# First block of a two-stage expert kernel in whole float32 products, halves of its weights made one block later

## The chip, the cores and the metric

The kernel runs on one NeuronCore of one Trainium2 chip. Its engines are TensorE (PE, matrix products into PSUM; PEld is its weight load), VectorE (DVE), ScalarE (ACT), GpSimd (POOL) and SyncE (SP), which issues all DMAs here. The metric is the device time of one execution in microseconds.

## The reference

Inputs are `x` (8 batches, 8 heads, 512 rows, 64 wide) and `state` (8, 8, 32, 64) in float32, and five weight matrices that arrive as float64. Three stages follow one another:

```python
scores = scale * x @ state^T;  a  = softmax(scores);   xread = a @ state      # per batch and head
scores2 = scale * state @ x^T; a2 = softmax(scores2);  sread = a2 @ x
x = concat([xread, sread]) regrouped to rows of 512     # 8 batches of 512 rows, 8 x 32 rows of state
x = (silu(x @ w_gate) * (x @ w_val)) @ w_out            # 512 -> 1536 -> 512
out = gelu_like(x @ w2_in) @ w2_out                     # 512 -> 2048 -> 512
```

The output is 4352 rows of 512 in float32.

## The kernel before

**Halves.** A float32 number is held as two tiles of TensorE's reduced type fp32r: the high half (a rounding copy by ACT) and the rest (a subtract by DVE or POOL). A product of two such pairs is three matmuls: high by high, low by high, high by low (`mm_rows`, L252 to L257; `mm_in`; `out1`, L699 to L701).

**Blocks.** The first layer runs over nine blocks: batches 0 to 6, then the 256 rows of the state ("tail"), then batch 7. A block has 12 steps `f`. A step makes one gate product (`gv`), SiLU on ACT, one value product, their product on DVE (`sg`), cuts that into halves `h`, and adds the step before it to four output accumulators (`out1`, 12 matmuls). For a batch, the softmax weights `a` are not first multiplied with the state: `state_weights` multiplies the state with a unit of the gate and value weights (tile `wu`, four units k = 0 to 3 for each pair of steps u), in two groups g of four heads, and its result (`xh`, `xl`) is what the step's products use. In words: unit, state weights, products. `coming` places the state weights of the next pair of steps.

**Weights.** `stream` lists all weight units in the order in which they are needed: 24 gate/value units and 12 output units ("o") in block 0, and the 12 output units again in every later block. A unit of float64 is loaded as raw words by SP (512 KB), turned to float32 by two ACT instructions (`w_begin`, L193 and L194), two on DVE and one add on POOL (`w_join`, L206 to L210), and cut into halves by an ACT copy and a POOL subtract (`w_end`, L221 and L222). The float32 form of the output units is stored to DRAM (`w1o`) and only cut again in later blocks. The second layer's 32 units are turned in the same way in blocks 1 to 6, one at every odd step ("turn"), and stored for later. Four raw buffers hold what is under way. `need(key)` runs the stream up to a key, in program order.

**Order.** Each engine runs its instructions in the order in which the program is written. `START` lists the work ahead of the first step (attention of batch 0 in groups A0 and A1, and the first four units); `BLOCK0` puts batch 1's attention (G0, G1) and batch 0's state read into block 0 at (step, place); `GROUP` does the same for later blocks. In block 0 `w_beside` places beginnings ("B") and ends ("E") of units between the parts of a step.

Of the kernel before, what the change touches and what calls it, by code (L numbers as in the profile page):

```python
# [20 lines left out]
A0.load0 state0 A0.load1 weights1 A0.turn0 A1.load0 attn_state A0.turn_h0 A1.load1 weights2 A0.turn1  # L21
A0.turn_l0:v A0.turn_h1 A0.turn_l1:v A0.scores_apart0 A0.scores_apart1 begin A1.turn0 A0.max_n
A1.turn_h0 weights3 A0.less_max:p A1.turn1 A1.turn_h1 A1.turn_l0:v end A0.exp_n A1.turn_l1:v
A0.sum_n begin weights4 A0.over_sum:v A0.back end A0.a_h:a A0.a_l:v A1.scores_apart0 begin
A1.scores_apart1 A1.max_n sw0 A1.less_max:v end A1.exp_n begin A1.sum_n weights4 A1.over_sum:v A1.back
A0.max_s A1.a_h:a A1.a_l:v A1.max_s end sw1 G0.load A1.exp_s A0.exp_s state1
# [6 lines left out]
    (0, 2): "A1.turn_e A0.cut_x:v",  # L33
    (1, 0): "G0.turn0 G0.turn_h0 G0.turn_l0:v",
    (1, 1): "A1.cut_x:v",
    (1, 2): "A0.state_read",
    (2, 0): "A0.state_sum",
    (2, 1): "attn_state",
    (2, 2): "A1.state_read A1.state_sum",
# [3 lines left out]
    (4, 2): "G0.max_s G0.cut_x:v G0.less_max:v",  # L43
    (5, 0): "G0.exp_n",
    (5, 1): "G0.exp_s G0.sum_n",
    (5, 2): "G0.over_sum:v G1.load G0.back G0.turn_e",
    (6, 1): "G0.a_h:a G0.a_l:v",
    (6, 2): "G0.state_read",
    (7, 1): "G1.turn0 G1.turn_h0 G1.turn_l0:v",
    (7, 2): "G0.state_sum",  # L50
    (8, 0): "G1.scores0 G0.state_store",
    (8, 1): "G1.turn1 G1.turn_h1 G1.turn_l1:v",
    (8, 2): "G1.scores1",
    (9, 0): "G1.cut_x:v",
    (9, 2): "G1.max_s G1.max_n G1.less_max:v",
    (10, 0): "G1.exp_n next",
# [23 lines left out]
def kernel(  # L80
# [74 lines left out]
    held = set()  # L155
    joins = []
    units = {}
    pos = {"dma": 0, "begun": 0, "done": 0, "ahead": 4, "apart": False}
    RAWS = 4

# [4 lines left out]
    def w_dma(ahead=None):  # L165
        ahead = ahead or pos["ahead"]
        while pos["dma"] < pos.get("limit", len(stream)) and len(raws) + len(held) < ahead:
            key, src, _, _ = stream[pos["dma"]]
            if isinstance(src, tuple):
# [12 lines left out]
    def w_begin():  # L182
# [4 lines left out]
        t = raw = raws.pop(key)  # L187
        if isinstance(src, tuple) or src.dtype != F32:
            r = raw.bitcast(U32).rearrange("p (c t) -> p c t", t=2)
            hi, lo = r[:, :, 1], r[:, :, 0]  # L190
            t = work.tile([P, DM], F32, name="wt", tag="wt", bufs=3)
            tu = t.bitcast(U32)
            a.activation(t, hi.bitcast(F32), ACTF.Copy, scale=2.0**-112)  # L193
            a.activation(lo, lo, ACTF.Copy, scale=2.0**-29)  # L194
            joins.append((tu, hi, lo))
            if not pos["apart"]:
                w_join()
        else:
            held.add(key)
        temps[key] = t  # L200
        pos["begun"] += 1

    def w_join():
        while joins:
            tu, hi, lo = joins.pop()
            v.tensor_scalar(out=tu, in0=tu, scalar1=3, scalar2=None, op0=ALU.logical_shift_left)  # L206
            v.scalar_tensor_tensor(  # L207
                out=tu, in0=hi, scalar=0x80000000, in1=tu, op0=ALU.bitwise_and, op1=ALU.bitwise_or
            )
            pool_e.tensor_tensor(tu, tu, lo, op=ALU.add)  # L210

    def w_end():
        key, src, loc, keep = stream[pos["done"]]
        t = temps.pop(key)
        if loc is None:
            sy.dma_start(keep, t)
            pos["done"] += 1
# [10 lines left out]

    def w_step(lead=2):
# [4 lines left out]
        while pos["begun"] < min(pos["done"] + lead, len(stream)):  # L234
# [55 lines left out]

    def load_state(b):
# [9 lines left out]
    def attn_state(b):  # L301
# [4 lines left out]
        t = stz[b % 2]  # L306
        a.copy(t[:, :, HIGHS], pv[:, :, :, 0])
# [5 lines left out]
    class Group:  # L313


        def __init__(self, b, g, slots=None):
            self.b, self.g, self.slots = b, g, slots or {}

# [16 lines left out]
        def turn(self, q):  # L335
# [6 lines left out]
            self.xt[q] = ps, self.tile(f"xth{q}", [P, S], F32R), self.tile(f"xtl{q}", [P, S], F32R)  # L342

        def turn_h(self, q):
            a.copy(self.xt[q][1], self.xt[q][0])

        def turn_l(self, q, eng):
            ps, xh, xl = self.xt[q]
# [12 lines left out]
        def scores_apart(self, q):  # L361

            ST, st, xh, xl = self.for_scores(q)
            ps = at()[0:64]
            hi, lo = st[:, (1 - q) * 64 : (2 - q) * 64], st[:, q * 64 : q * 64 + 64]
            pe.matmul(ps, hi, xh, start=True, stop=False)
            pe.matmul(ps, lo, xh, start=False, stop=False)
            pe.matmul(ps, hi, xl, start=False, stop=True)
            a.copy(ST, ps)
# [54 lines left out]

        def a_h(self, eng):
            self.a = (ae, ao)[self.b % 2].tile([P, 2, S], F32R, name="a", tag=f"a{self.g}")
# [5 lines left out]
        def turn_e(self):  # L432
            self.ec = self.tile("ec", [P, J, 4, 64], F32R)
            ps = at()
            for j in range(J):
                pe.transpose(ps[:, j * P : (j + 1) * P], self.e2[:, j * P : (j + 1) * P], ident)
            cut(self.ec[:, :, 0:4:3], self.ec[:, :, 1:3], ps.rearrange("p (j q m) -> p j q m", j=J, q=2))

        def state_read(self):


            ps = at()
            for q in range(2):
# [10 lines left out]
        def state_sum(self):  # L454
            sm, ps = self.sm, self.sr
            low = ap.tile([P, P], F32, name="low", tag="low")
            self.srd = srd = ap.tile([P, D], F32, name="srd", tag="srd", bufs=2)
# [26 lines left out]
    def state_weights(b, u, g):  # L484
# [3 lines left out]
        pairs = []  # L488
        for q in range(2):
            sh, sl = (stz[b % 2][:, g, i + q : i + q + 2].rearrange("p c m -> p (c m)") for i in (1, 5))  # L490
# [6 lines left out]
    def mm_state(ps, b, f, t):  # L497

        c = slice(t * 2 * P + f % 2 * P, t * 2 * P + f % 2 * P + P)
        pairs = []  # L500
        for g in range(2):
# [12 lines left out]
    def plan_batch(plan, b):  # L514
# [11 lines left out]
        more = {"attn_state": lambda: attn_state(b), "next": load_next}  # L526
        if b == 1:
# [16 lines left out]
    def add_gv(u, k):  # L544
        r, c = slice(k * P, (k + 1) * P), slice(u * 2 * P, (u + 1) * 2 * P)
        add(("gv", u, k), (w_gate[r, c], w_val[r, c]), (wp, f"w{u * KD + k}", 1))
# [29 lines left out]
    for f in range(F1):  # L576
        add(("o", NB1 - 1, f), w1o[f], (wp, "o", 2))
        add(*next(rest), (wp, f"w{2 * f}", 1))
        add(*next(rest), (wp, f"w{2 * f + 1}", 1))
# [25 lines left out]
    def h_tile(n):  # L605
# [5 lines left out]
    names = ["xn", "xc0", "xc1", "xth0", "xtl0", "xth1", "xtl1", "ST", "sp", "aT", "e2", "ec"]  # L611
    far = {n: f"w{2 * F1 - 1 - i}" for i, n in enumerate(names)}
    A0 = Group(0, 0, {n: f"w{2 * F1 - 1 - len(names) - i}" for i, n in enumerate(["xn", "aT", "xth1", "xtl1"])})
    A1 = Group(0, 1, far)
    xop = {}
    groups[0, 0], groups[0, 1] = A0, A1
    groups[1, 0] = Group(1, 0)
# [3 lines left out]
        "begin": w_begin,  # L621
        "end": w_end,
# [41 lines left out]
    for i, blk in enumerate(order1):  # L664
# [5 lines left out]
        pos["apart"] = i > 0  # L670
# [19 lines left out]
        def out1(f, between=None, k0=0):  # L690
            if not acc:
                acc.extend(accs())
            need(("o", i, f))
            h = hs.pop(f)
            w = units.pop(("o", i, f))
            for e in range(KD):
                c = slice(e * P, (e + 1) * P)
                ps = acc[e][:, :N]
# [166 lines left out]
```

## Time and profile before

| | |
|---|---|
| three runs | 1671.36, 1671.38, 1673.2 us, median 1671.38 |
| profiled execution | 1668.41 us, span of the core 1666.6 us |
| PE busy | 1569.8 us of the span |
| mean granted clock of TensorE | 0.974 |

A span is the time from the first to the last instruction. The clock is given as a share of full speed (2.4 GHz). A matmul's row shows its latency; since matmuls follow one another in a pipeline, the price of one in a run of them is the distance from start to start.

### The profile page before, as it was taken

What the parts mean: (1) busy time and instruction counts of PE and PEld (TensorE: products, weight loads), DVE (VectorE), ACT (ScalarE), POOL (GpSimd) and SP (SyncE); (2) the same over time, 40 slices, a digit from 0 to 9 for tenths busy, and PEclk for the clock granted to TensorE, in tenths of its full rate; (3) what the DMA queues carried; (4) which work ended last, traced back from release to release, by engine and by line L of the source; (5) the groups of instructions that cost most, each with busy time, mean ns of one, the idle gap of its engine ahead of it and who ended that gap; (6) DMA issues with size and microseconds to landing.
All of it is one profiled execution on the core that took longest, in us unless ns stands there. A gap on an engine that the chain in (4) does not pass through costs nothing.

```text
span 1666.6 us, 18801 instructions
## 1 busy us (share of the span) xinstructions
PE 1569.8 (94%) x7100; PEld 1275.7 (77%) x7100; DVE 751.5 (45%) x1253; ACT 683.8 (41%) x1218; POOL 355.8 (21%) x263
## 2 busy tenths in 40 slices
PE   5677899999989999999999999999999999999997
PEld 3456677787777778779988888888888888888886
DVE  5787666564656666463233223222222222322222
ACT  5575555554545555454355222222222222222222
POOL 3565333233323323223354010000000000000000
PEclk7787899999999999999999999999999999999999
DMA  5345333423333343323243001010101010000000
GB/s 145 127 138 149 105 104 98 125 82 122 103 111 109 89 124 100 101 64 98 81 142 124 32 1 51 1 45 7 45 7 39 13 38 13 32 20 29 10 26 13
DMA packets 94963, 119.18 MB, mean 72 GB/s; under 512 B 45209, under 2 KB 54425, under 8 KB 94873
## 3 DMA queue, kind: packets, MB, share of 16 engines
q1 hardware_dynamic: 94872, 117.99, 23.4%
q8 instruction: 55, 0.90, 0.2%
q14 instruction: 36, 0.29, 0.1%
HBM read 88.08 MB, written 29.88 MB: 71 GB/s over the span
## 4 chain that ended last, share of the span: by engine, by line
PE 50%; DVE 0%; issue 0%
PE gv L250 8%; PE gv L249 8%; PE gv L248 8%; PE acc L261 7%; PE acc L260 7%; PE acc L262 7%; PE acc L701 1%; PE acc L700 1%; PE acc L699 1%; PE gv L256 1%; PE gv L255 1%; PE gv L257 1%; PE at L255 0%; PE at L256 0%; PE at L257 0%; DVE ev L602 0%
## 5 line engine op out<-in xcount | busy, mean ns | idle before, releaser
L826 DVE TENSOR_TENSOR sg<-gv,sg 128x512 f32<-128x512 f32 (+1 forms) x144 | 95.3, 662 | 433.3 <-ACT sg L825 433.3
L825 ACT ACTIVATE sg<-gv 128x512 f32<-128x512 f32 (+1 forms) x144 | 82.6, 573 | 447.3 <-PE gv L250 447.3
L222 POOL TENSOR_TENSOR wu<-raw,wu 128x512 fp32r<-128x512 f32 x128 | 178.8, 1402 | 278.5 <-ACT wu L221 203.0
L250 PE MATMUL gv<-xl,wu 128*128 128x512 f32 (+1 forms) x576 | 219.6, 381 | 0.0
L249 PE MATMUL gv<-xh,wu 128*128 128x512 f32 (+1 forms) x576 | 219.2, 381 | 0.0
L248 PE MATMUL gv<-xh,wu 128*128 128x512 f32 (+1 forms) x576 | 218.9, 380 | 0.0
L261 PE MATMUL acc<-wu,h 128*128 128x512 f32 x544 | 213.2, 392 | 0.0
L260 PE MATMUL acc<-wu,h 128*128 128x512 f32 x544 | 212.9, 391 | 0.0
L262 PE MATMUL acc<-wu,h 128*128 128x512 f32 x544 | 212.1, 390 | 0.0
L256 PE MATMUL gv<-a,xl 128*128 128x512 f32 x384 | 158.7, 413 | 15.7 <-DVE xl L590 12.4
L700 PE MATMUL acc<-h,wu 128*128 128x512 f32 (+1 forms) x432 | 166.1, 384 | 6.3 <-POOL wu L222 6.3
L699 PE MATMUL acc<-h,wu 128*128 128x512 f32 (+1 forms) x432 | 166.9, 386 | 0.0
L701 PE MATMUL acc<-h,wu 128*128 128x512 f32 (+1 forms) x432 | 165.1, 382 | 1.0 <-DVE h L757 0.9
L255 PE MATMUL gv<-a,xh 128*128 128x512 f32 x384 | 159.6, 416 | 0.5 <-ACT xh L589 0.5
L210 POOL TENSOR_TENSOR wt<-wt,raw 128x512 uint32<-128x512 uint32 x68 | 92.0, 1352 | 313.4 <-DVE wt L207 183.8
L257 PE MATMUL gv<-a,xh 128*128 128x512 f32 x384 | 157.3, 410 | 0.0
L590 DVE TENSOR_TENSOR h<-sg,h 128x512 fp32r<-128x512 f32 (+1 forms) x144 | 95.4, 663 | 95.4 <-ACT h L589 90.8
L589 ACT CAST h<-sg 128x512 fp32r<-128x512 f32 (+1 forms) x144 | 86.0, 597 | 104.9 <-DVE sg L826 104.9
L738 ACT ACTIVATE sg<-gv 128x512 f32<-128x512 f32 (+1 forms) x108 | 62.1, 575 | 159.7 <-PE gv L257 159.5
L248 PEld LDWEIGHTS gv<-xh,wu 128*128 128x128 f32 x576 | 108.3, 188 | 22.3
L249 PEld LDWEIGHTS gv<-xh,wu 128*128 128x128 f32 x576 | 108.1, 188 | 22.3
L250 PEld LDWEIGHTS gv<-xl,wu 128*128 128x128 f32 x576 | 108.3, 188 | 21.8
(105 smaller groups left out, 2590.7 us busy)
## 6 DMA issues: line engine op xcount, KB each, us to landing
raw<-w1o SPq DMA_DIRECT2D x96, 256.0 KB
raw<-in_moe_w_out_dram SPq DMA_DIRECT2D x28, 512.0 KB
raw<-in_moe_w_in_dram SPq DMA_DIRECT2D x16, 512.0 KB
y<-ev SPq DMA_DIRECT2D x16, 512.0 KB
xr<-y SPq DMA_DIRECT2D x32, 256.0 KB
out_dram<-ev SPq DMA_DIRECT2D x16, 512.0 KB
xn<-in_x_dram SPq DMA_DIRECT2D x14, 512.0 KB
raw<-in_moe_w_gate_dram SPq DMA_DIRECT2D x24, 256.0 KB
```

What stands on the lines that cost most here:

```text
L222: pool_e.tensor_tensor(u[:, 1, :], t, f32(u[:, 0, :]), op=ALU.subtract)
L248: pe.matmul(ps[:, :N], wh, xh, start=k == 0, stop=False)
L249: pe.matmul(ps[:, :N], wl, xh, start=False, stop=False)
L250: pe.matmul(ps[:, :N], wh, xl, start=False, stop=k == KD - 1)
L255: pe.matmul(ps, wh, xh, start=k == 0, stop=False)
L256: pe.matmul(ps, wl, xh, start=False, stop=False)
L260: pe.matmul(ps, lh, rh, start=first, stop=False)
L261: pe.matmul(ps, lh, rl, start=False, stop=False)
L262: pe.matmul(ps, ll, rh, start=False, stop=last)
L699: pe.matmul(ps, w[:, 0, c], h[:, 0, :N], start=f == 0, stop=False)
L700: pe.matmul(ps, w[:, 1, c], h[:, 0, :N], start=False, stop=False)
L701: pe.matmul(ps, w[:, 0, c], h[:, 1, :N], start=False, stop=f == F1 - 1)
```

## The change

In block 0 the products take float32 tiles as they are (`mm_whole`): one matmul instruction where there were three, and no halves are made of the units, of the state weights, of `a` or of `h`. That holds for the scores and the state read of batch 0 too (and for the state read of batch 1's first group). Units are begun and merged by `whole_slot`, three times a step; two gate/value units share one old slot of the halves. The halves of these 24 units are made later by `cut_unit` (one ACT copy, one POOL subtract): the first four in steps 8 to 10 of block 0, the other 20 in block 1, called from `coming` by `need(("cut", ...))`. State weights of the next pair are made ahead of the value product at odd steps and after it at even ones, as in later blocks. The second layer's units are turned at steps 3 to 9 of blocks 2 to 6, seven a block, and not at odd steps from block 1 on. `START` issues the loads of two weight units ahead of `x`.

```diff
 START = """
-A0.load0 state0 A0.load1 weights1 A0.turn0 A1.load0 attn_state A0.turn_h0 A1.load1 weights2 A0.turn1
-A0.turn_l0:v A0.turn_h1 A0.turn_l1:v A0.scores_apart0 A0.scores_apart1 begin A1.turn0 A0.max_n
...
+weights2 A0.load0 state0 A0.load1 A1.load0 A1.load1 weights4 A0.turn0 attn_state A0.turn_h0 A0.turn1
+A0.turn_h1 A0.scores_full slot A1.turn0 A1.turn_h0 A1.turn1 A1.turn_h1 A0.max_n slot A0.less_max:v
...
 BLOCK0 = {
...
-    (8, 0): "G1.scores0 G0.state_store",
+    (8, 0): "G1.scores0 G0.state_store cut_w0",
...
+    def cut_unit(u, k):
+        n = u * KD + k
+        t = whole[n]
+        if n == 2 * F1 - 1:
+            t = work.tile([P, DM], F32, name="wt", tag="wt", bufs=3)
+            a.copy(t, whole[n])
+        units["gv", u, k] = w = wp.tile([P, 2, DM], F32R, name="wu", tag=f"w{home(n)}", bufs=1)
+        a.copy(w[:, 0, :], t)
+        pool_e.tensor_tensor(w[:, 1, :], t, f32(w[:, 0, :]), op=ALU.subtract)
+
+    def whole_slot():
+        n = pos["begun"]
+        older = bool(joins)
+        if n <= where["o", 0, F1 - 1] and stream[n][0] in raws:
...
+                w_turn(t, raw)
...
+        if older:
+            key, _, _, keep = stream[pos["done"]]
+            tu, hi, lo = joins.pop(0)
+            w_merge(tu, hi, lo)
+            if keep is not None:
+                sy.dma_start(keep, units[key])
...
+        w_dma()
...
+    def mm_whole(ps, pairs):
+        for k, (w, x_) in enumerate(pairs):
+            pe.matmul(ps, w, x_, start=k == 0, stop=k == len(pairs) - 1)
...
         ps = at()
         pairs = []
+        if b == 0:
+            mm_whole(
+                ps,
+                [(groups[b, g].columns(q)[0], whole[u * KD + 2 * g + q]) for q in range(2)],
+            )
+            sw[b, u, g] = t = x_tiles(xp, u % 2 * 2 + g, DM)
+            (v.tensor_copy if g else a.copy)(f32(t[0]), ps)
+            return
...
     for i in range(1, NB1 - 2):
         for f in range(F1):
+            if i == 1 and f % 2 == 0 and f + 2 < F1:
+                for k in range(2):
+                    add(("cut", f // 2 + 1, k), None, "place")
             add(("o", i, f), w1o[f], (wp, "o", 2))
+            if i == 1 and f % 2 == 0 and f + 2 < F1:
+                for k in range(2, KD):
+                    add(("cut", f // 2 + 1, k), None, "place")
-            turn = next(turns, None) if f % 2 else None
+            turn = next(turns, None) if i > 1 and f in range(3, 10) else None
...
+                if i == 0:
+                    pe.matmul(ps, w[:, c], f32(h[:, 0, :N]), start=f == 0, stop=f == F1 - 1)
...
             if u < U1 and not tail:
-                need(("gv", u, 2 * g + 1))
+                if i == 0:
+                    need_whole(("gv", u, 2 * g + 1))
+                if i == 1:
+                    need(("cut", u, 2 * g + 1))
                 state_weights(blk, u, g)
```

**PE in block 0.** Before, one output accumulator takes three matmuls, from the halves `wu`; here two of the four of a step, and the state product of the next units after them.

```order
L699 MATMUL acc_523<-h,wu 128x512
L700 MATMUL acc_523<-h,wu 128x512
L701 MATMUL acc_523<-h,wu 128x512
L699 MATMUL acc_524<-h,wu 128x512
L700 MATMUL acc_524<-h,wu 128x512
L701 MATMUL acc_524<-h,wu 128x512
```

After, a state product (from the whole unit `wf`), a gate or value product and the four accumulators of a step follow one another in eight instructions.

```order
L325 MATMUL at<-wf,st_101 128x512 x2
L325 MATMUL gv<-a,xh 128x512 x2
L825 MATMUL acc_425<-h,wt 128x512
L825 MATMUL acc_426<-h,wt 128x512
L825 MATMUL acc_427<-h,wt 128x512
L825 MATMUL acc_428<-h,wt 128x512
```

Each of these instructions reads float32 as it is, where the ones before read halves.

**ACT in block 1, step 1.** Before, behind the SiLU (L738) and the scores' copy (L358) comes the copy of the state weights (`xh`), which the product of the next unit needs.

```order
L738 ACTIVATE sg<-gv 128x512
L358 COPY ST<-at 64x512
L589 CAST xh<-at 128x512
L221 CAST wu<-raw 128x512
L345 CAST xth_1638<-at 128x512
```

After (SiLU is L864, scores L436), two high halves (L252, from the whole units `wf`) stand between them, and PE's state product of this step is what makes `at` for `xh`.

```order
L864 ACTIVATE sg<-gv 128x512
L436 COPY ST<-at 64x512
L252 CAST wu<-wf 128x512 x2
L715 CAST xh<-at 128x512
L236 CAST wu<-raw 128x512
L422 CAST xth_1179<-at 128x512
```

The two copies moved into block 1 stand behind the SiLU of their own step, and ahead of what reads the product that they feed.

**ACT in block 2, step 0.** Before, a turn (L193, L194) stands between the output unit's copy and the copy of the turned `x` (`xth`).

```order
L738 ACTIVATE sg<-gv 128x512
L307 CAST stz_96<-at 128x2x2x64
L309 COPY stz_96<-stz_96 128x2x2x64
L221 CAST wu<-raw 128x512
L193 ACTIVATE wt<-raw 128x512
L194 ACTIVATE raw<-raw 128x512
L345 CAST xth_2407<-at 128x512
```

After, at the same place (L422 is the copy of the turned `x`):

```order
L864 ACTIVATE sg<-gv 128x512
L381 CAST stz_96<-at 128x2x2x64
L383 COPY stz_96<-stz_96 128x2x2x64
L236 CAST wu<-raw 128x512
L422 CAST xth_1947<-at 128x512
```

The turn is gone from here; in these blocks the first one now stands in step 3.

## Rows read from the trace of the kernel before

**Rows 1.** The page, parts 1 and 2: engines over the span, granted clock in 40 slices

```profile
PE 1569.8 (94%) x7100; PEld 1275.7 (77%) x7100; DVE 751.5 (45%) x1253; ACT 683.8 (41%) x1218; POOL 355.8 (21%) x263
...
PEclk7787899999999999999999999999999999999999
```

**Rows 2.** Windows by stage: us, busy of each engine (instructions), clock, DMA share, GB/s

```profile
0.00:36.20 36.20, 16.74 (x44) 8.92 (x45) 22.30 (x38) 16.34 (x28) 12.53 (x15) 0.77 0.56 160
36.20:200.05 163.85, 121.39 (x437) 90.15 (x436) 122.66 (x185) 101.23 (x181) 88.85 (x64) 0.80 0.41 125
200.05:294.57 94.52, 91.40 (x413) 73.50 (x412) 58.28 (x105) 52.37 (x93) 31.36 (x22) 1.00 0.35 103
294.57:770.44 475.87, 453.68 (x2058) 365.89 (x2056) 287.19 (x517) 254.94 (x452) 149.12 (x106) 1.00 0.34 101
```

**Rows 3.** Waits of PE, 0 to 36.2 us: total us, times, longest us

```profile
PE at L255 <- ACT wu L221: 10.4, 3, 4.9
```

**Rows 4.** Waits of PE, 36.2 to 200.05 us

```profile
PE gv L256 <- DVE xl L590: 12.4, 4, 3.8
PE at L255 <- DVE ec L590: 6.0, 1, 6.0
PE at L257 <- POOL wu L222: 5.5, 3, 2.3
```

**Rows 5.** Timeline of PE at block 1: start us, us, instruction

```profile
200.05 0.39 PE L255 MATMUL gv<-a,xh 128*128 128x512 f32 x1
...
201.22 0.40 PE L257 MATMUL gv<-a,xh 128*128 128x512 f32 x1
...
211.05 0.60 PE L339 MATMUL at<-ident,xn 128*128 128x128 f32 x4
211.41 0.48 PE L699 MATMUL acc<-h,wu 128*128 128x512 f32 x1
```

**Rows 6.** Groups by line, 36.2 to 200.05 us: count, busy us, mean ns, idle before

```profile
L222 POOL TENSOR_TENSOR wu<-wt,wu 128x512 fp32r<-128x512 f32 x32 | 45.3, 1414 | 14.8 <-ACT wu L221 14.8
L210 POOL TENSOR_TENSOR wt<-wt,raw 128x512 uint32<-128x512 uint32 x32 | 44.5, 1391 | 50.7 <-DVE wt L207 18.2 <-issue 10.3 <-ACT wu L221 6.1
L207 DVE SCALAR_TENSOR_TENSOR wt<-raw,wt 128x512 uint32<-128x512 uint32 x32 | 30.8, 961 | 1.2
...
L206 DVE TENSOR_SCALAR wt<-wt 128x512 uint32<-128x512 uint32 x32 | 25.0, 782 | 18.8 <-ACT wt L193 18.6
...
L193 ACT ACTIVATE wt<-raw 128x512 f32<-128x512 f32 x32 | 21.7, 677 | 12.7 <-POOL wu L222 11.4 <-DMA w1o<-wt 0.9
```

**Rows 7.** Timeline of ACT in block 1

```profile
216.37 0.60 ACT L738 ACTIVATE sg<-gv 128x512 f32<-128x512 f32 x1 [0.88 <-PE gv L257]
216.86 0.61 ACT L221 CAST wu<-raw 128x512 fp32r<-128x512 f32 x1
217.37 0.66 ACT L193 ACTIVATE wt<-raw 128x512 f32<-128x512 f32 x1
...
223.90 1.28 ACT L411 ACT_TABLE_LOAD   x1
...
226.44 0.56 ACT L589 CAST xh<-at 128x512 fp32r<-128x512 f32 x1
```

**Rows 8.** Groups by line on POOL, 200.05 to 294.57 us

```profile
L222 POOL TENSOR_TENSOR wu<-raw,wu 128x512 fp32r<-128x512 f32 x12 | 17.8, 1482 | 24.3 <-ACT wu L221 24.3
```

**Rows 9.** Timeline of POOL in block 1

```profile
217.55 1.31 POOL L222 TENSOR_TENSOR wu<-raw,wu 128x512 fp32r<-128x512 f32 x1 [2.17 <-ACT wu L221]
```

**Rows 10.** Waits of PE, 294.57 to 770.44 us (blocks 2 to 6)

```profile
PE at L356 <- DVE xtl L349: 10.8, 5, 3.0
PE at L445 <- DVE ec L590: 6.6, 5, 1.3
PE acc L700 <- POOL wu L222: 4.7, 4, 1.2
```

**Rows 11.** Timeline of ACT in block 2, step 0

```profile
300.82 0.66 ACT L193 ACTIVATE wt<-raw 128x512 f32<-128x512 f32 x1 [2.37 <-DMA raw<-in_moe_w_in_dram]
```

More of the change, by code (lines that the diff above doesn't have):

```diff
@@ L227, in w_end, with need_whole @@
         pos["done"] += 1
+    def cut_unit(u, k):
[11 more added lines that the diff above has]
+        if n <= where["o", 0, F1 - 1] and stream[n][0] in raws:
+            key = stream[n][0]
+            if key[0] == "gv" or key[2] - 3 < pos["outs"]:
+                raw = raws.pop(key)
+                if key[0] == "o":
+                    units[key] = t = work.tile([P, DM], F32, name="wt", tag="wt", bufs=3)
+                else:
+                    m = key[1] * KD + key[2]
+                    if m % 2 == 0:
+                        pairs_of["now"] = wp.tile([P, 2, DM], F32, name="wf", tag=f"w{m // 2}", bufs=1)
+                    whole[m] = t = pairs_of["now"][:, m % 2, :]
+                w_turn(t, raw)
+                held.add(key)
+                pos["begun"] += 1
+        if older:
[4 more added lines that the diff above has]
+                sy.dma_start(keep, units[key])
+            held.discard(key)
+            pos["done"] += 1
+        w_dma()
+    def need_whole(key):
+        while pos["done"] <= where[key]:
+            before = pos["done"], pos["begun"]
+            whole_slot()
+            assert before != (pos["done"], pos["begun"]), key
     def w_step(lead=2):
@@ L359, in scores, with scores_full, columns @@
             v.tensor_tensor(ST, ps[0:64], ST, op=ALU.add)
[L361 to L369, printed above, removed]
+        def scores_full(self):
+            ps = at()
+            mm_whole(ps, [(self.columns(q)[0], f32(self.xt[q][1])) for q in range(2)])
+            self.ST = self.tile("ST", [P, S])
+            a.copy(self.ST, ps)
+        def columns(self, q):
+            if self.b == 0:
+                return [st0[:, self.g, q : q + 2].rearrange("p c m -> p (c m)")]
+            st = stz[self.b % 2][:, self.g]
+            return [st[:, i + q : i + q + 2].rearrange("p c m -> p (c m)") for i in (1, 5)]
         def for_scores(self, q):
@@ L442, in state_read @@
             ps = at()
+            if self.whole:
+                xs = [self.xn[:, j].rearrange("p h d -> p (h d)") for j in range(J)]
+                mm_whole(ps[:, : 4 * D], [(self.ec[:, j * P : (j + 1) * P], xs[j]) for j in range(J)])
+                self.sr = ps
+                return
             for q in range(2):
@@ L500, in mm_state @@
         pairs = []
+        if b == 0:
+            mm_whole(ps, [(f32(sw[b, f // 2, g][0])[:, c], f32(groups[b, g].a[:, 0])) for g in range(2)])
+            return
         for g in range(2):
@@ L526, in plan_batch @@
         more = {"attn_state": lambda: attn_state(b), "next": load_next}
+        for k in range(KD):
+            more[f"cut_w{k}"] = lambda k=k: cut_unit(0, k)
         if b == 1:
@@ L577 @@
         add(("o", NB1 - 1, f), w1o[f], (wp, "o", 2))
-        add(*next(rest), (wp, f"w{2 * f}", 1))
-        add(*next(rest), (wp, f"w{2 * f + 1}", 1))
+        add(*next(rest), (wp, f"w{home(2 * f)}", 1))
+        add(*next(rest), (wp, f"w{home(2 * f + 1)}", 1))
     add(*next(rest), (wp, "o", 2))
@@ L703, in out1, with beside @@
                     between(k0 + e // 2)
-        def w_beside(ops):
-            for op in ops if i == 0 else "":
-                if op == "E":
-                    if pos["begun"] > pos["done"] and pos["done"] < where["o", 1, 0]:
-                        w_end()
-                    continue
-                w_dma()
-                if pos["begun"] < min(pos["done"] + 2, len(stream)) and stream[pos["begun"]][0] in raws:
-                    w_begin()
-                    w_dma()
+        def beside():
+            if i == 0:
+                whole_slot()
         def product(ps, f, t):
@@ L747 @@
             product(pv, f, 1)
-            w_beside("B")
-            v.tensor_tensor(sg[:, :N], pv[:, :N], sg[:, :N], op=ALU.mult)
+            beside()
+            h = h_tile(f % 2)
+            if i == 0:
+                v.tensor_tensor(f32(h[:, 0, :N]), pv[:, :N], sg[:, :N], op=ALU.mult)
+            else:
+                v.tensor_tensor(sg[:, :N], pv[:, :N], sg[:, :N], op=ALU.mult)
             run(f, 1)
-            if f % 2 == 0 and i > 0:
+            if f % 2 == 0:
                 coming(f, 0)
-            w_beside("EB" if early_ else "E")
-            h = h_tile(f % 2)
-            a.copy(h[:, 0, :N], sg[:, :N])
-            w_beside("B")
-            v.tensor_tensor(h[:, 1, :N], sg[:, :N], f32(h[:, 0, :N]), op=ALU.subtract)
+            if i > 0:
+                cut(h[:, 0, :N], h[:, 1, :N], sg[:, :N])
             hs[f] = h
-            w_beside("E" if early_ else "")
             if last:
@@ L763 @@
                 out1(f - 1, nxt, 0) if f == F1 - 1 else out1(f - 1)
+            beside()
             run(f, 2)
-            w_beside("BB" if early_ else "B")
-            if i == 0:
-                coming(f, f % 2)
-            elif stream[pos["done"]][2] is None:
+            if i > 0 and stream[pos["done"]][2] is None:
                 w_step()
```

156 lines of the change are left out of this document (98 added, 58 removed).

## The prediction

> **What bounds the kernel now.** I read the page first. PE is busy 94% of the span, and its clock is granted in full in all slices but the first five, of 41.7 us each [rows 1]: what is to be won lies at the start. The windows by stage say where: ahead of the first step (36.2 us) and in block 0 (163.85 us) PE is busy for 17 and 121 us at a clock of 0.77 and 0.80, in block 1 for 91.4 of 94.5 us at full clock, and so in blocks 2 to 6 [rows 2]. So block 0 is not bound by PE's work, and everything later nearly is. In the waits of PE in block 0 the reader is to see what ends last: low halves of state weights (12.4 us), of turned exponentials (6.0) and of units (5.5) [rows 4]; ahead of block 0 it is the units' high halves, 10.4 us [rows 3]. A half comes late because of the chain that makes it, not because an engine is full: POOL, the longest link, works 89 of 164 us [rows 2].
>
> **The price of a product.** In a run of half products the distance is 1.17 us over five, 0.234 us each [rows 5]. No row shows a product of float32 as such. From below, it is one instruction, 0.234 us. The only float32 matmuls here are transposings, four in 0.36 us, 0.09 each for 128 columns [rows 5]; 512 columns would be 0.36, 1.54 half products. If each of four passes were that long, it would be 1.44, the upper end. I take four passes, 0.936 us: three half products are what the same result costs now, and they leave out low by low. That is nearest to the row of the same tiles. The Trainium skill (FP8 and Floating Point Precision, TensorE Precision Notes) gives true float32 four passes, high and low of both sides each with each; by it the price is 0.94 as well, and no row here shows it.
>
> **Block 0, before 163.85 us.** Its products after: 48 of gate and value (12 steps x 2 x 2), 48 of the output (12 x 4), 20 of state weights (5 pairs of steps x 4), 116 x 0.936 = 108.6 us. Beside them 12 state-read products of 256 columns (half of 0.936, 5.6 us), 8 scores and 12 half products of block 1's first state weights (20 x 0.234 = 4.7), G1's state read (8 x 0.117 = 0.9), nine groups of four transposings (9 x 0.36 = 3.2). Sum 123 us, 10 a step. Does anything else need longer? A step turns three units: on POOL 3 x 1.39 = 4.2 us, on DVE 3 x (0.78 + 0.96) = 5.2 and some 3 us of products and attention, on ACT three pairs at 0.68 each, 4.1, and a SiLU of 0.6 [rows 6, 7]. The 32 low halves on POOL (45.3 us) and as many copies on ACT are gone [rows 6]. So PE bounds this block, and the units come from slots one to two ahead of their use. I add 4 us for a first stretch at half clock and 5 us for three or four waits of the attention pieces that stay (the three waits for POOL in [rows 4] are 1.8 each on the mean): 132 us. Minus 32. At one pass PE is no bound; what is left is DVE's 8 us a step, 98 us in all, minus 66; at 1.44 the products take 58 us more, plus 26.
>
> **Ahead of block 0.** The wait for units' high halves (10.4 us) [rows 3] bounds the gain, and 1 MB of weights now ahead of `x` the loss: at the 160 GB/s of this stretch [rows 2] 6.5 us. On DVE four low halves of x, two of `a` and two of state weights go, three merges of units come, and the second state weights' copy, for which the first product waits, stands behind all of them. I take minus 2.
>
> **Block 1, the new wait.** 20 units are cut here. A cut stands behind its step's SiLU on ACT, which waits for the gate product, and PE's next work at an odd step is the state product that reads the halves. From the end of the gate product: the SiLU 0.1 us later, the first copy 0.49 after it, the second 0.51 later [rows 7]; POOL starts 0.69 after a copy [rows 7, 9] and takes 1.48 for each [rows 8], so the second low half is there at 4.24 us. PE's next matmul can start 0.17 us before that end, since a row of 0.40 is followed after 0.234 [rows 5]; it would be through with its six at 1.23 and is through at 4.5: 3.3 us. At an even step a value product (1.4 us) lies between: 1.9 us. Five of each are 26 us. At steps 3 and 8 a table load and two exponentials stand between SiLU and copies, 2.54 us each [rows 7]: +5. The last unit's copy waits for POOL: +0.5. At step 4 a state read fills the wait (-1.9), and two waits that block 1 has now, as blocks 2 to 6 have them (1.3 and 1.2 us, [rows 10]), fall into the new ones: 27 us. Behind the waiting copies ACT holds the output unit's copy, the state weights' copy and `h`'s; all are needed a step later. Behind the waiting state product PE holds all that follows, so nothing hides these waits. Bounds: 15 us, if only POOL's subtracts are seen (10 x 1.48), to 27 and a clock that falls as well.
>
> **The clock there.** The row to hold against it is the wait of 3.0 us in blocks 2 to 6 [rows 10], where the granted clock stays 1.00 [rows 2]; but there such waits come once a block, here at every step. I take 4 us. The Trainium skill (TensorE: Matmul & The Clock Gate, HAM oscillation — how this bites in real kernels) warns that waits between bursts of matmuls bring the throttle back again and again. By that rule block 1 would be like block 0; what this would cost, from rows, is the third rival. Together block 1: plus 31.
>
> **Blocks 2 to 6.** A turn in step 0 waits 2.37 us on ACT for its load [rows 11], the turned x behind it is late, and PE waits for its low half, 10.8 us in five blocks; the subtract for the last output unit stands behind a turn's add on POOL, 4.7 us [rows 10]. Turns at steps 3 to 9 are past both places: their loads stand behind more output units on SP, their stores too, and nothing of them is left when the block ends. Minus 15.5. The seventh turn and those at even steps put two ACT, two DVE and one POOL instruction and two DMAs where none were: +3.5, up to 6.6 if the waits for `ec` double. Minus 12, between -15.5 and +7. Block 1 loses its six turns, all of them off its path.
>
> **Sum.** -2 - 32 + 31 - 12 = -15 us. The profiled execution took 1668.4 us (span 1666.6), so 1653.4; the median of the runs is 3.0 above it, so 1656.
>
> **The rivals.**
> 1. Float32 products dearer than four passes. For: the transposings take 1.54 of a half product per column, and no row shows the thing itself. Against: a weight load lies beside a matmul throughout (PEld 77%, PE 94% [rows 1]). The point is 15 / 116 = 0.13 us more, 1.07 each; from there it is slower. At 1.44: +58, 1714 us.
> 2. Feeding still bounds block 0. For: raw buffers stay four, DVE's merges grew to 1.7 us under load [rows 6]. Against: half of POOL's work is gone. The point is a step of 12.3 us; at the present 13.65 it would be +32, 1688 us.
> 3. The clock falls in block 1 as in block 0: 91.4 us of work at 0.80 [rows 2] is 22.9 us more, in place of 4: 1675 us.
> 4. The halves in block 1 are not late, since ACT and POOL run ahead; 8 us in place of 31: 1633 us. Against: the order on ACT puts the copies behind the SiLU.
>
> **How the numbers follow.** The forecast has 0.52, and by itself 1643 to 1668; rivals 1 to 4 have 0.13, 0.12, 0.10 and 0.13. A change under 0.2% (3.3 us) can't be told from none here. Faster: nearly all of the forecast, rival 4, a little of 2 and 3: 0.65. Slower: most of 1, over half of 2, half of 3: 0.23. The rest, 0.12, is no change. The range reaches from rival 4 to between rivals 3 and 2, 1632 to 1682; a dear product lies outside.
>
> **What would show it.** Right: products in block 0 at 0.9 to 0.95 us from start to start, steps of some 10.5 us, the clock near 1 after the first; in block 1 waits of PE for POOL's low halves and ACT's copies, at each of ten steps, 25 to 30 us, and block 1 at 120 to 127 us; no wait for `xtl` nor for POOL's output half in blocks 2 to 6. Wrong: products above 1.07 us, waits of PE in block 0 for merges on POOL, a clock below 0.9 in block 1, or a block 1 under 105 us.

## The result

The changed kernel takes 1626.4 us in the median of four runs (1623.6 to 1627.2), the kernel before 1671.4 in the runs beside them: a ratio of 0.973, 95% interval 0.971 to 0.975. The forecast was 1656 with a range of 1632 to 1682. The sign was right; the size was a third of what came, and the time lies outside the range.

### The profile page after: what moved, and what is told of

Same layout as the page of the kernel before. It is cut to its first block, busy times and chain, and to the rows that moved or that the text cites. A ratio compares the mean times of both kernels' runs of the same rounds, so it can differ in the third digit from the quotient of the medians.

```text
span 1621.8 us, 18423 instructions
## 1 busy us (share of the span) xinstructions
PE 1570.9 (97%) x6976; PEld 1244.9 (77%) x6976; DVE 734.7 (45%) x1209; ACT 660.0 (41%) x1172; POOL 325.5 (20%) x250
## 4 chain that ended last, share of the span: by engine, by line
PE 51%; DVE 0%; issue 0%
PE gv L313 8%; PE gv L312 8%; PE gv L311 8%; PE acc L329 8%; PE acc L328 8%; PE acc L330 8%; PE acc L831 1%; PE acc L830 1%; PE acc L829 1%; PE gv L319 1%; PE gv L318 1%; PE gv L320 1%; PE at L318 0%; PE at L319 0%; PE at L320 0%; DVE ev L728 0%
## 5 line engine op out<-in xcount | busy, mean ns | idle before, releaser
L947 ACT ACTIVATE sg<-gv 128x512 f32<-128x512 f32 (+1 forms) x144 | 82.6, 573 | 447.3 <-PE gv L313 447.3
L237 POOL TENSOR_TENSOR wu<-raw,wu 128x512 fp32r<-128x512 f32 x128 | 169.1, 1326 | 309.5 <-ACT wu L236 241.5
L716 DVE TENSOR_TENSOR h<-sg,h 128x512 fp32r<-128x512 f32 (+1 forms) x240 | 171.4, 714 | 115.6 <-ACT h L715 109.0
L715 ACT CAST h<-sg 128x512 fp32r<-128x512 f32 (+1 forms) x240 | 143.0, 596 | 160.6 <-DVE sg L948 104.9
L829 PE MATMUL acc<-h,wu 128*128 128x512 f32 (+1 forms) x384 | 146.5, 382 | 0.0
L831 PE MATMUL acc<-h,wu 128*128 128x512 f32 (+1 forms) x384 | 145.3, 378 | 0.1
L830 PE MATMUL acc<-h,wu 128*128 128x512 f32 (+1 forms) x384 | 145.2, 378 | 0.0
L318 PE MATMUL gv<-a,xh 128*128 128x512 f32 x336 | 136.5, 406 | 0.0
L319 PE MATMUL gv<-a,xl 128*128 128x512 f32 x336 | 134.1, 399 | 0.0
L320 PE MATMUL gv<-a,xh 128*128 128x512 f32 x336 | 133.7, 398 | 0.0
L330 PEld LDWEIGHTS acc<-wu,h 128*128 128x128 f32 x544 | 102.1, 188 | 22.4
L328 PEld LDWEIGHTS acc<-wu,h 128*128 128x128 f32 x544 | 102.1, 188 | 22.5
```

The costliest lines, as they stand in the source:

```text
L237: pool_e.tensor_tensor(u[:, 1, :], t, f32(u[:, 0, :]), op=ALU.subtract)
L328: pe.matmul(ps, lh, rh, start=first, stop=False)
L330: pe.matmul(ps, ll, rh, start=False, stop=last)
L716: v.tensor_tensor(l_, src, f32(h_), op=ALU.subtract)
L829: pe.matmul(ps, w[:, 0, c], h[:, 0, :N], start=f == 0, stop=False)
L830: pe.matmul(ps, w[:, 1, c], h[:, 0, :N], start=False, stop=False)
```

## The profile after

The profiled execution has a span of 1621.8 us. From the page, PE's busy time and the clock in 40 slices, which answer to [rows 1]:

```profile
PE 1570.9 (97%) x6976; PEld 1244.9 (77%) x6976; DVE 734.7 (45%) x1209; ACT 660.0 (41%) x1172; POOL 325.5 (20%) x250
...
PEclk9999999999999999999999999999999999999999
```

PE's busy time is that of before in sum (1569.8) and the span 45 us shorter: in sum, the time came out of PE's idle time. By stage the busy time did move: block 1 has 14 us more of it, the stages around it 13 less. The windows by stage say where, cut at the first gate product of a block, as in [rows 2]; the columns are the same (stage, its length, busy us of PE, PEld, DVE, ACT and POOL, granted clock, DMA share, GB/s). The last row is all that follows block 6.

```profile
0.00:28.83 28.83, 13.88 (x37) 6.47 (x37) 17.81 (x29) 14.08 (x25) 6.50 (x10) 0.92 0.59 175
28.83:150.11 121.28, 115.71 (x321) 56.61 (x320) 88.29 (x151) 68.08 (x119) 47.72 (x36) 0.99 0.54 171
150.11:276.36 126.25, 105.46 (x414) 77.27 (x413) 52.84 (x93) 56.72 (x102) 46.89 (x36) 0.92 0.15 44
276.36:725.62 449.26, 449.26 (x2057) 367.29 (x2056) 314.33 (x529) 262.26 (x464) 150.56 (x112) 1.00 0.38 117
725.62:1621.80 896.18, 886.57 (x4155) 737.28 (x4153) 261.40 (x408) 258.90 (x465) 73.87 (x56) 1.00 0.12 39
```

Against [rows 2], with the forecast beside it:

| stage | before | after | change | forecast |
|---|---|---|---|---|
| ahead of block 0 | 36.2 | 28.8 | -7.4 | -2 |
| block 0 | 163.9 | 121.3 | -42.6 | -32 |
| block 1 | 94.5 | 126.3 | +31.7 | +31 |
| blocks 2 to 6 | 475.9 | 449.3 | -26.6 | -12 |
| the rest | 896.2 | 896.2 | 0.0 | 0 |

What answers to [rows 4] and [rows 10], the waits of PE (line waited at, who was waited for; total us, times, longest us), is in block 0:

```profile
PE gv L325 <- DVE xh L602: 2.3, 1, 2.3
PE at L325 <- DVE xtl L427: 2.1, 1, 2.1
PE at L325 <- DVE ST L437: 1.2, 1, 1.2
```

and in block 1:

```profile
PE at L318 <- ACT wu L252: 13.2, 8, 3.9
PE at L320 <- POOL wu L253: 7.3, 15, 0.7
```

In blocks 2 to 6 none is left, and PE is busy for all 449.26 us at full clock. A block of that kind takes 90.22 us; this is the floor against which block 1 is held below.

The price of a float32 product stands in the timeline of PE in block 0 (start, length, instruction; each product shows as two records, so `x8` is four products of 512 columns; the view ends in the third row):

```profile
78.72 3.60 PE L825 MATMUL acc<-h,wt 128*128 128x512 f32 x8
82.16 1.88 PE L325 MATMUL gv<-a,xh 128*128 128x512 f32 x4
83.87 0.59 PE L325 MATMUL at<-wf,st 128*128 128x512 f32 x1
```

From start to start four products take 3.44 us and two 1.71: 0.86 us each. The forecast had 0.936, four half products of 0.234 [rows 5].

Block 1's worst step shows the mechanism that the forecast worked out for it. ACT:

```profile
179.46 0.60 ACT L864 ACTIVATE sg<-gv 128x512 f32<-128x512 f32 x1 [2.07 <-PE gv L320]
180.06 1.28 ACT L493 ACT_TABLE_LOAD   x1
...
182.07 0.61 ACT L488 ACTIVATE sp<-sp 128x512 f32<-128x512 f32 x1
182.59 1.12 ACT L252 CAST wu<-wf 128x512 fp32r<-128x512 f32 x2
```

and PE, at the state product that reads the halves:

```profile
183.25 0.80 PE L318 MATMUL at<-wu,stz 128*128 128x512 f32 x1 [3.89 <-ACT wu L252]
183.84 0.63 PE L319 MATMUL at<-wu,stz 128*128 128x512 f32 x1
```

The two copies of the cut stand behind the SiLU, a table load and the exponentials. The matmul after the wait lasts 0.80 and the next 0.63 us, where a row at full clock has 0.40: the clock has fallen to its lower level. The windows of 2 us around it (columns as above; the next to last three figures are the clock, the DMA share and GB/s) show what PE did before:

```profile
178.00:180.00 2.00, 1.36 (x6) 0.75 (x4) 0.00 (x0) 0.54 (x1) 1.55 (x2) 1.00 0.02 8
180.00:182.00 2.00, 0.00 (x0) 0.00 (x0) 0.00 (x0) 1.98 (x4) 0.00 (x0) 0.84 0.00 0
182.00:184.00 2.00, 0.75 (x2) 0.50 (x2) 0.00 (x0) 1.71 (x5) 0.73 (x1) 0.50 0.00 0
...
186.00:188.00 2.00, 2.00 (x6) 1.62 (x6) 0.67 (x1) 1.10 (x2) 0.11 (x1) 0.50 0.00 0
188.00:190.00 2.00, 2.00 (x9) 1.60 (x9) 1.16 (x3) 0.41 (x1) 1.17 (x1) 0.95 0.00 0
```

It falls in a stretch in which PE does nothing, and PE, at work again from 183, works at 0.50 until 188.

## The experiments

My theory after the result: block 0 is bound by PE at 0.86 us a product; block 1's loss is only the place of the cuts behind the SiLU; blocks 2 to 6 gain because the turns left the steps where x is turned. Stages are cut as above in every run. The runs with one time only (e4 to e7 and e9) are read by their stages; in blocks 2 to 6 six runs with the change's turns (the changed kernel, e1 and e6 to e9) agree to 0.1 us.

**e1_turns_only.** The kernel before with the turns' part of the change alone, their places and the new rule of when one is begun:

```diff
-            turn = next(turns, None) if f % 2 else None
+            turn = next(turns, None) if i > 1 and f in range(3, 10) else None
...
-        while pos["begun"] < min(pos["done"] + lead, len(stream)):
+        while pos["begun"] < len(stream):
+            if pos["begun"] >= pos["done"] + (lead if stream[pos["begun"]][2] else 1):
+                break
```

> The kernel before with one part of the change alone: the turns of second-layer units stand at steps 3 to 9 of blocks 2 to 6 (none in block 1), and a turn is begun only when it is the next in the stream. Theory T (the turns alone made the 26.6 us that blocks 2 to 6 lost, since PE no longer waits for xtl, ec and POOL there and refills its pipeline less often): blocks 2 to 6 at 448 to 452 us instead of 475.9, block 1 1 to 3 us shorter since its six turns are gone, the whole at 1641 to 1647 us against 1671. Rival R (only the waits for xtl and POOL's output half go, as the prediction had it, and the rest comes from what block 1 leaves behind in the changed kernel): blocks 2 to 6 at 462 to 466 us, the whole at 1657 to 1661.

1638.7 us (1637.7 to 1639.8), ratio 0.980 [0.979, 0.982]. By stages, block 1 and then blocks 2 to 6:

```profile
199.94:290.16 90.22, 90.22 (x413) 73.81 (x412) 51.36 (x93) 45.25 (x81) 21.48 (x16) 1.00 0.22 61
290.16:739.39 449.23, 449.23 (x2058) 367.41 (x2056) 313.19 (x529) 262.50 (x464) 151.02 (x112) 1.00 0.39 117
```

Blocks 2 to 6 have the time of the changed kernel to 0.03 us, so nothing that block 1 leaves behind plays a part: R falls. Block 1 itself is 4.3 us shorter without its six turns, more than the 1 to 3 expected. The turns' part is worth 32.7 us, over twice the whole gain that was forecast.

**e2_turns_odd.** The changed kernel with the turns at odd steps again (two of them in block 1, so that all 32 find a place), the new rule of beginning kept:

```diff
-            turn = next(turns, None) if i > 1 and f in range(3, 10) else None
+            turn = next(turns, None) if (i > 1 or f >= 9) and f % 2 else None
```

> The changed kernel with the turns put back at odd steps of blocks 2 to 6 (and at steps 9 and 11 of block 1, so that all 32 find a place), all else as changed; the rule that a turn is begun only when it is next stays. Theory T (the place of the turns makes the whole of the gain there): waits of PE for xtl come back and blocks 2 to 6 take 470 to 477 us, the whole 20 to 28 us above the changed kernel, 1646 to 1654. Rival R (the place is worth the 15.5 us of the two waits alone): 12 to 16 us above it, 1638 to 1642. Rival Q (the rule on when a turn is begun makes the gain, not the place): 0 to 6 us above it.

1626.6 us, the changed kernel's time; blocks 2 to 6 take 450.1:

```profile
278.17:728.26 450.09, 449.40 (x2057) 367.30 (x2056) 302.98 (x525) 257.06 (x460) 146.91 (x110) 1.00 0.38 113
```

My theory falls here: the place was put back and the gain stayed. Rival Q holds. In the kernel before, ACT waited in those blocks for the turns' loads:

```profile
ACT wt L193 <- DMA raw<-in_moe_w_in_dram: 15.8, 9, 3.3
ACT wt L193 <- DMA raw<-in_moe_w_out_dram: 3.7, 5, 1.1
```

In e2 it waits for no DMA there, though the turns stand where they stood.

**e5_turns_begun_early.** The fourth cell: the new place with the old rule, which lets a turn's conversions begin one step ahead of its own.

```diff
-            if pos["begun"] >= pos["done"] + (lead if stream[pos["begun"]][2] else 1):
+            if pos["begun"] >= pos["done"] + lead:
```

> The changed kernel, turns at steps 3 to 9, with the old rule of when a turn is begun: up to two units ahead, so that its two conversions on ACT are issued one step before its own. With the kernel before (odd steps, old rule: 475.9 us in blocks 2 to 6), the changed one (steps 3 to 9, new rule: 449.3) and e2_turns_odd (odd steps, new rule: 450.1) it is the fourth cell of two by two. Theory Q (the rule made the gain, by beginning a turn only when its load is there and merging it behind h's cut on DVE; the place would also do part of it): waits for ec at least come back, blocks 2 to 6 at 455 to 466 us. Rival P (either alone is enough): 449 to 451 us. Rival N (the place does nothing at all): 472 to 478 us.

Blocks 2 to 6 take 459.1 us, within Q's 455 to 466:

```profile
278.29:737.39 459.10, 451.48 (x2057) 366.66 (x2056) 301.84 (x529) 263.16 (x464) 156.94 (x112) 1.00 0.39 115
```

So, in us:

| | old rule | new rule |
|---|---|---|
| odd steps | 475.9 | 450.1 |
| steps 3 to 9 | 459.1 | 449.3 |

The place alone is worth 16.8, the rule alone 25.8, both 26.6: the rule does all that the place does, and 9 us more. (The cells do not hold equally many turns: 26 in the kernel before, 30 in e2, 32 in the other two; the rest stand in block 1.) What the 9 us are is in the waits of PE in e5:

```profile
PE at L543 <- DVE ec L716: 6.7, 5, 1.3
PE at L318 <- DVE xl L716: 0.9, 4, 0.2
```

The wait for the turned exponentials has stayed as it was [rows 10]. DVE in block 2 of e5 shows why:

```profile
304.02 0.69 DVE L716 TENSOR_TENSOR xl<-at,xh 128x512 fp32r<-128x512 f32 x1 [5.67 <-ACT xh L715]
304.63 0.42 DVE L217 TENSOR_SCALAR wt<-wt 128x512 uint32<-128x512 uint32 x1
305.08 0.69 DVE L218 SCALAR_TENSOR_TENSOR wt<-raw,wt 128x512 uint32<-128x512 uint32 x1
305.69 0.68 DVE L877 TENSOR_TENSOR sg<-gv,sg 128x512 f32<-128x512 f32 x1
...
307.52 1.45 DVE L501 TENSOR_TENSOR sp<-sp,sq 128x512 f32<-128x512 f32 x1
...
309.49 0.68 DVE L716 TENSOR_TENSOR ec<-at,ec 128x512 fp32r<-128x512 f32 x1
```

and in the changed kernel, the same step of the same block:

```profile
302.10 0.69 DVE L716 TENSOR_TENSOR xl<-at,xh 128x512 fp32r<-128x512 f32 x1 [5.67 <-ACT xh L715]
302.71 0.68 DVE L877 TENSOR_TENSOR sg<-gv,sg 128x512 f32<-128x512 f32 x1
...
304.51 0.69 DVE L501 TENSOR_TENSOR sp<-sp,sq 128x512 f32<-128x512 f32 x1
...
305.72 0.68 DVE L716 TENSOR_TENSOR ec<-at,ec 128x512 fp32r<-128x512 f32 x1
306.32 0.42 DVE L217 TENSOR_SCALAR wt<-wt 128x512 uint32<-128x512 uint32 x1
```

With the old rule a turn's merge stands ahead of the product of `h`, with the new one behind the subtract for `ec`. From the subtract for `xl` to that for `ec` it is 5.47 us in e5 and 3.62 here: 1.85 later. Of these 1.06 are the merge itself (304.63 to 305.69), and 0.76 are the softmax product `sp` at L501, which takes 1.45 us in e5 and 0.69 here. In e5 POOL is at work beside it, since the last add of the merge, also POOL's, has held up its subtract for the output unit:

```profile
307.11 1.30 POOL L237 TENSOR_TENSOR wu<-raw,wu 128x512 fp32r<-128x512 f32 x1
```

In the changed kernel that subtract ran ahead of `sp`, from 302.67. PE waits 1.3 us for `ec` in e5, once a block.

**e3_cuts_early.** The changed kernel with block 1's cuts issued one place earlier, ahead of the next step's SiLU on ACT:

```diff
             run(f, 2)
+            u = (f + 1) // 2 + 1
+            if i == 1 and u < U1:
+                need(("cut", u, 1 if f % 2 else 3))
...
         out1(F1 - 1, nxt, 2)
+        if i == 0:
+            need(("cut", 1, 1))
```

> The changed kernel with block 1's cuts of gate and value units issued one place earlier: at the end of the step before, ahead of the next step's SiLU on ACT, where now they stand behind it (the first two right after block 0's last output products). Same instructions, another order on ACT and POOL. Theory T (the new waits in block 1 are only the place behind the SiLU, and the clock there falls only for those waits): PE's waits for ACT's and POOL's halves fall from 20.5 us to under 4, the clock in block 1 is 0.98 to 1.00, block 1 takes 96 to 102 us instead of 126, the whole 24 to 30 us below the changed kernel, 1597 to 1602. Rival C (the waits go, the clock stays at about 0.92): block 1 at 103 to 108 us, the whole 18 to 23 us below. Rival M (ACT and POOL have no room, the copies now hold up the SiLU or the product of h): block 1 at 112 to 122 us, 4 to 14 us below.

1598.5 us (1597.8 to 1600.1), ratio 0.956 [0.955, 0.958] to the kernel before: 28 us below the changed kernel, as T said. Block 1:

```profile
151.91:252.82 100.91, 95.65 (x415) 73.97 (x413) 54.61 (x93) 55.97 (x100) 44.93 (x34) 0.98 0.19 55
```

and all of PE's waits there:

```profile
PE at L320 <- POOL wu L253: 5.1, 10, 1.1
```

The waits fell from 20.5 to 5.1 us (a little over T's 4), those for ACT are gone, and the clock came back with them, 0.92 to 0.98: rival C, a clock that stays down, falls, and so does M.

**e8_cuts_earlier.** The cuts another step ahead (four behind block 0's last output products, then two at the end of each step for the step after the next), and in the work ahead of block 0 the copy of the second state weights ahead of the row maxima. Against e3_cuts_early (the stream of block 1's units is put in the same order):

```diff
-slot sw0 A1.sum_n A1.over_sum:v A1.back_full slot A0.max_s A1.max_s slot sw1 G0.load A1.exp_s A0.exp_s
+slot sw0 A1.sum_n A1.over_sum:v A1.back_full slot sw1 A0.max_s A1.max_s slot G0.load A1.exp_s A0.exp_s
...
-            u = (f + 1) // 2 + 1
+            u = f // 2 + 2
-                need(("cut", u, 1 if f % 2 else 3))
+                need(("cut", u, 3 if f % 2 else 1))
```

> The changed kernel with block 1's cuts a whole step further ahead than in e3_cuts_early (four right after block 0's last output products, then two at the end of each step for the step after the next), and with the copy of block 0's second state weights issued on DVE ahead of the two row maxima and a unit's merge, for which the second gate product waited 2.3 to 3.3 us. Theory T (block 1's loss is only where the cuts stand): the ten waits for POOL of 5.1 us in e3_cuts_early go, with them the one fall of the clock, block 1 at 91 to 95 us instead of 100.9; the wait for the copy shrinks to under 1 us. The whole 8 to 12 us below e3_cuts_early, 1587 to 1591 us. Rival M (the earlier cuts hold up block 0's eviction or POOL's other work): block 1 at 98 to 104 us, the whole at 1594 to 1602.

1592.9 us (1592.2 to 1594.6), ratio 0.953 [0.952, 0.954]: the fastest version, 33 us below the changed kernel, a little above the 1587 to 1591 that T gave. Block 1, and all of PE's waits in it:

```profile
151.83:246.34 94.51, 92.53 (x415) 74.95 (x413) 55.11 (x94) 54.66 (x98) 42.44 (x32) 0.98 0.21 59
```

```profile
PE at L318 <- DVE xl L716: 2.0, 1, 2.0
```

No wait for a cut is left. The other edit gave nothing that can be seen: the wait of 2.8 us for the copy that e3 has is gone, but PE now waits 2.3 us in block 0 for ACT's copy of the first turned exponentials, which stands behind a SiLU and a unit's conversions there, and up to the end of block 0 both need the same time, 151.83 and 151.91 us. One wait took the place of another.

**e4_less_products and e7_more_products.** Block 0 with 20 of its 48 output products left out, and with the same 20 issued twice:

```diff
+                    if not (e >= 2 and 0 < f < F1 - 1):
...
+                    for _ in range(2 if e >= 2 and 0 < f < F1 - 1 else 1):
```

> The changed kernel without 20 of block 0's 48 output products (the upper two column groups in steps 1 to 10 are left out, so block 0's result is incomplete). Theory T (block 0 is bound by PE, at 0.86 us a product): 20 x 0.86 = 17.2 us less, of which 14 to 17.5 show, block 0 at 104 to 107 us. Rival F (block 0 is bound by the units' merges and turns on DVE, POOL and ACT): block 0 stays at 116 to 121 us, and PE waits for the units in place of its products.

> The changed kernel with 20 of block 0's output products issued twice (the upper two column groups in steps 1 to 10, so that these sums hold them twice). Theory T (block 0 is bound by PE, a float32 product of 512 columns takes 0.86 us wherever it stands): 20 x 0.86 = 17.2 us more, block 0 at 137 to 139 us. Rival F (part of it lies in waits that block 0 has): 10 to 14 us more. Rival O (the forecast's price, 0.936): 18.7 us more.

Block 0, e4 and then e7:

```profile
30.07:138.04 107.97, 101.28 (x282) 50.04 (x280) 88.14 (x151) 68.52 (x119) 47.16 (x36) 0.97 0.62 192
28.92:170.80 141.88, 134.72 (x362) 65.18 (x360) 87.51 (x151) 67.96 (x119) 47.17 (x36) 0.98 0.47 146
```

That is 13.3 less and 20.6 more than 121.28, where 20 products are 17.2. By the stage's time rival O, 18.7, is nearer to e7 than T is; the timeline decides between their prices. In e7 the timeline of PE has six products from 62.27 to 67.42:

```profile
62.27 5.31 PE L826 MATMUL acc<-h,wt 128*128 128x512 f32 x12
67.42 1.88 PE L325 MATMUL gv<-a,xh 128*128 128x512 f32 x4
```

which is 0.858 each: T's price holds, and O's 0.936 falls. Most of the other 3.4 us lies in block 0's first 30 us: the wait for `xtl` is 3.3 there where it was 2.1, and from 49 to 59 us the clock is 0.85, where the changed kernel had 1.00. In e4 the clock over block 0 is 0.97 against 0.99 (0.67 in its first 10 us, where the changed kernel had 0.89), and it waits 6.7 us in place of 5.6, most of the 3.9 that are missing. Both numbers are outside T's bounds, on the same side; but F, a block bound by its feed, asked for at most some 5 us less in e4 and falls. Block 0 is bound by PE, except at its start.

**e6_x_first and e9_start_halves.** Two looks at the work ahead of block 0: the loads with all of x ahead of the units (before, one unit stood between; the leading `weights2` left out, so that `weights4` behind `A1.load1` loads all), and the halves of the first four units made again in tiles that nothing reads:

```diff
-weights2 A0.load0 state0 A0.load1 A1.load0 A1.load1 weights4 A0.turn0
+A0.load0 state0 A0.load1 A1.load0 A1.load1 weights4 A0.turn0
```

```diff
+            if key[0] == "gv" and key[1] == 0:
+                w = wp.tile([P, 2, DM], F32R, name="wu", tag=f"w{home(key[2] % 2)}", bufs=1)
+                a.copy(w[:, 0, :], tu.bitcast(F32))
+                pool_e.tensor_tensor(w[:, 1, :], tu.bitcast(F32), f32(w[:, 0, :]), op=ALU.subtract)
```

> The changed kernel with the loads ahead of block 0 in the old order: x and the state first, then the units' loads. Two runs of the changed order reached the first gate product at 28.8 and 29.7 us, and two more with the same start at 30.5 and 30.1; x's first transposing stood at 7.57 us, in the kernel before at 4.63. Theory S (leaving the halves away made the gain ahead of block 0; the units' merges on DVE and POOL bind, so that units landing later cost): first transposing at 4.5 to 5 us, first gate product at 29 to 34 us. Rival X (x's chain binds): 2 to 3 us earlier, 26 to 27.5 us. Rival L (the order of loads made the whole gain): 35 to 37 us.

> The changed kernel with the first four units' halves made again ahead of block 0, besides: behind the merge of each, a copy on ACT and a subtract on POOL into tiles that nothing reads. Everything else as changed, x's and a's halves stay away. Before, PE waited 10.4 us for units' halves ahead of block 0; now 5.4 us for the whole units. Five runs with the changed start and the changed order of loads reached the first gate product at 28.8 to 30.5 us. Theory S (POOL's subtracts and ACT's copies stood in the units' chain, each 1.3 to 1.5 us on POOL: four of them, of which three lie ahead of the last state weights): first gate product 3 to 6 us later, 32.5 to 36 us. Rival H (it is the products of halves and x's and a's halves that went, the units' chain has room): 28.5 to 31 us.

The first gate product stood at 28.07 us in e6 and at 32.56 in e9. Six runs with the changed start lie between 28.8 and 30.5, 29.8 in the middle. With x first its transposing starts at 5.00 us and not at 7.54, but the first gate product comes only 0.8 to 2.5 us earlier. The new order of loads therefore gained nothing and cost 2.5 us at most; e6 lies between its own S and X, so it does not show which chain binds. The halves of four units cost 2 to 4 us. Of the 5.7 to 7.4 us that the stage gained, this is what the runs tell apart, from one run each; whether the rest came with x's and `a`'s halves or with the smaller number of products was not separated.

## Why the prediction was wrong

**Blocks 2 to 6, "Minus 12, between -15.5 and +7": this step failed, by 14.6 us.** The waits for `xtl` and for POOL, priced at 15.5, did go with the place (16.8 in e5). But the step priced only the table of places. The change also has a line in `w_step` (e1 shows it) by which a turn is begun only when all units before it are done, and not while one is still open; I gave that line no cost and no gain. It is worth 9.8 us on top of the place, and 25.8 without it. Three terms make up the 14.6. The waits for `ec`, 6.6 us, which I let stay, went with the rule: by the two timelines of DVE above, because the merge then stands behind `ec`. PE's busy time fell from 453.7 to 449.3 us, 4.4 us over the 14 waits of [rows 10], 0.3 each, where I had counted the wait alone: a row of 0.40 ends 0.17 us after the next could have started, and the first matmul behind a wait is followed after 0.34 us, not 0.234 (303.27 to 303.61, at the end of this text). The 3.5 us for added turns were not seen at all: they stand beside a PE that waits for nothing.

**Block 0, "132 us": the limit was right, two sizes were not.** PE bounds it, and rivals 1 and 2 are out. The product came at 0.86, not 0.936: 116 x 0.076 = 8.8 us. That is 3.67 half products of 0.234, not four; why it is less than four was not tried. The Trainium skill (FP8 and Floating Point Precision, TensorE Precision Notes) gives four passes for true float32; the 0.86 is near to it, and rules out one pass. The 4 us for a half clock were about 1 (0.89 in the first 10 us and 1.00 after, where [rows 2] had 0.80 for the whole block); the 5 us of waits were 5.6.

**Ahead of block 0, "minus 2".** It lay between the 10.4 us of [rows 3] on one side and 6.5 us of loads on the other. The loads were priced too high: PE's wait for x grew from 5.5 to 7.8 us, and by e6 the whole stage lost 2.5 at most. The waits for units fell from 11.4 to 5.4 us, and PE's busy time from 16.7 to 13.9, a term that the sum did not have.

**Block 1, "plus 31".** The stage came out at +31.7, but not by its terms; that the number came true is luck. Against the floor of 90.22 us the 126.25 hold 20.5 us of waits (forecast 29.6, which less 2.5 are its 27: nearly two thirds are for ACT's copies, and POOL's subtracts then run behind PE's first matmuls) and 15.2 of PE's busy time beyond the floor, at half clock or in restarting (forecast 4). From the whole 4.3 go off for the six turns that left, where I took 2.5. Too much waiting and too little clock cancelled. e3 and e8 show that the mechanism was right: with the cuts ahead of the SiLU 25 us go, and a step more brings block 1 to 94.5. On rival 3, the Trainium skill (TensorE: Matmul & The Clock Gate, HAM oscillation — how this bites in real kernels) says that waits between bursts bring the throttle back; the trace agrees in kind, at a clock of 0.92 and not block 0's old 0.80, and in e8, with no cut to wait for, the only dip left in block 1 follows one wait of 2.0 us for `xl`.

**The sum.** 1656 less 5.4, 10.6 and 14.6, plus 0.7, is 1626. Three misses had one sign, for more than one reason: a line of the change without a price, a product and loads priced too high. What a wait costs behind it, beyond its length, is in two of them, with 4.4 us in blocks 2 to 6 and some 3 of clock in block 0. Rival 4, the one that lay near the measured time, was wrong in its reason: it had block 1 at 8 us more, and that took 31.7.

## What to carry to other kernels

- A change of when a unit is begun, one line in a helper, can outweigh the table of places that it comes with: price every line of the diff that moves an instruction on a shared engine, and look at what then stands ahead of what (here a merge of 1.1 us ahead of `h` on DVE).
- A wait of PE costs more than its length: some 0.3 us each in blocks 2 to 6 here, and behind some waits (3.9 us in block 1, 1.99 in e8) half the clock for some microseconds.
- Look for work that feeds PE and stands behind an instruction that itself waits for PE: here, moving the cuts ahead of the SiLU, with no instruction less, gave 28 us, and a step more together with it 33.

## What the hardware showed unexpectedly

A float32 matmul shows as two records, and its 512 columns take 0.86 us from start to start, less than the four half products by which I priced it.

The softmax product `sp` on DVE (L501, in the kernel before L419) has two lengths. In blocks 2 to 6 of the kernel before, of the changed kernel, of e2 and of e5 it took 1.42 to 1.45 us the 14 times that an instruction of POOL ran beside it, and 0.69 the 26 times that none did: here the work of one engine lengthened another's, with no wait between them in the profile.

And two waits of the same length left the clock in two ways. PE in block 2 of the kernel before:

```profile
303.27 0.50 PE L356 MATMUL at<-xth,stz 128*128 128x512 f32 x1 [2.05 <-DVE xtl L349]
303.61 0.40 PE L357 MATMUL at<-xtl,stz 128*128 128x512 f32 x1
```

and in block 1 of e8:

```profile
221.56 0.50 PE L318 MATMUL at<-wu,stz 128*128 128x512 f32 x1 [1.99 <-DVE xl L716]
221.90 0.40 PE L319 MATMUL at<-wu,stz 128*128 128x512 f32 x1
...
222.63 0.63 PE L319 MATMUL at<-wu,stz 128*128 128x512 f32 x1
```

After 2.05 us the matmuls stayed at 0.40 us and the windows around it at 1.00; after 1.99 us they went to 0.63 a microsecond later, and the clock to 0.50 from 223 to 225. What decides between the two was not tried.
